# A hand-written order of steps replaced by another, with nine row subtractions moved from VectorE to GpSimd

## The chip, the cores and the metric

The kernel runs on one core of a Trainium2 chip. What counts is the device time of one execution in microseconds (us), the median of three runs. The engines of the core are TensorE (PE in the rows; its weight loads are PEld), VectorE (DVE), ScalarE (ACT), GpSimd (POOL) and SyncE (SP, which here only issues transfers).

## The reference

Four batches, eight heads of width 64 and 768 positions go through attention with a window of 128 and 4 sink positions; the 3072 rows that come out, 512 wide, go through a feed-forward layer with 2048 hidden units and a squared ReLU.

```python
scores = scale * np.matmul(q, k.transpose(0, 1, 3, 2))
keep = is_sink | in_window                      # rel in [0, window)
a = np.exp(np.where(keep, scores, -1e9) - max); a = a / (a.sum(-1) + 1e-9)
x = np.matmul(a, v)                             # (B, S, H*D) rows
h = np.maximum(x @ w_in, 0.0)
return h * h @ w_out
```

The weights arrive as float64, so that the kernel reads them as pairs of 32-bit words and makes of each row tile a high and a low part.

## The kernel before, in words

**Tiles.** A chunk is half a sequence: 384 positions, three query blocks of 128; there are eight chunks. A pair is two heads of one chunk; a chunk has four pairs. The pairs of chunks 0 and 1 are numbered 0 to 7.

**Attention of a pair.** Six score products (two heads, three blocks) go from TensorE into a bank of PSUM (`s`, line 277). VectorE scales, masks and takes a row bound (line 298), ScalarE takes the exponential and its sum (line 301). ScalarE adds a small number to the six sums and VectorE inverts them (309, 310). GpSimd multiplies the probabilities by the inverses, three instructions to a head (331), and packs the sink columns (344, 345). TensorE transposes the probabilities into three banks (`pt`, 408) and the sink columns into another (`pss`, 352); ScalarE or VectorE copies them to SBUF (`PTF`, 416, and `SK`, 359). TensorE makes the value product (`xo`, 462 and 465), ScalarE copies its high part (474), and VectorE subtracts for the low part (478).

**Feed-forward.** For each of 16 blocks of hidden units there are 12 matmuls into `ph` (524), ReLU and squares on ScalarE (535 to 540), a low part `gl` on VectorE (547), and 9 matmuls into `po` (562). Half a leg (one chunk, eight blocks) is cut into 32 quanta. For the first leg the order writes them as p0 to p31: two quanta of `ph`, then one of two thirds and one of a third of the `po` of the block before. p2 and p3 hold no matmul, so that p0 to p31 make eight `ph` and seven `po`.

**Rows of weights.** There are 32 row tiles; up to row 24, row 0 and the odd ones are of `w_in` (blocks 0, 1, 2, ...), the other even ones of `w_out` (blocks 0, 1, ...). VectorE makes a row in four steps: A (line 628), B (630), C (632, followed by ScalarE's copy of the high part, 637) and D, the low part (641): a subtraction of two tiles of SBUF, 128x512. A raw row lies in one of four buffers, and the load of row n+4 waits until step C of row n has read it.

**Order.** Up to the last step of that first leg the order on TensorE, VectorE, ScalarE, GpSimd and SyncE is written out by hand, as a string of small steps (`SCHEDULE`), and each engine does its share of them strictly in that order. A step's first letter says what it is, the first digit the pair: `s` scores, `x` the rest of a score, `e` inverses, `z` scaling of one head, `t` and `c` transposes and their copies, `k` and `K` the same for the sink columns, `m` value product, `X` and `L` its high and low part, `q` `v` `w` loads of queries and keys, of values and of a row, `A` to `D` a row's steps, `p` a quantum. A last `a` or `d` is the engine of a copy, `@n` the bank. `i` is a number of idle matmuls, 128x512 on zeros (line 684), whose result nobody reads. After the string the order comes from a planner that the change does not touch: from chunk 1's first feed-forward product on, TensorE's rows are the same in both kernels but for names and line numbers.

Of the kernel before, what the change touches and what calls it, by code (L numbers as in the profile page):

```python
# [50 lines left out]
K5a w12 D9 x701 C10 A11 m5 s702@3 B11 x702 s711@1 s712@0 D10 p17 p18 C11 A12 x712 k6@0 x711 B12 C12
t61@1 w13 D11 p19 w14 p20 w15 e7 v6 A13 c61a p21 D12 t62@2 K6a B13 c62a t60@1 z70 p22 A14 B14 z71
C13 w16 c60a p23 D13 w17 X5a p24 t70@1 C14 t72@3 A15 L5 p25 k7@0 w18 m6 c70a D14 c72a p26 B15 p27
C15 t71@1 X6a A16 c71a K7a L6 B16 p28 C16 v7 p29 D15 m7 p30 X7a p31 L7 D16
"""

# [6 lines left out]
def sink_window_attention_moe(  # L63
# [25 lines left out]
    with ExitStack() as fast:  # L89
# [18 lines left out]
        idle = ap1.tile([P, 512], BF16, tag="KS1", name="idle")  # L108
# [140 lines left out]
        def bank(b, name):  # L249
            pool, tag = ((ps_att, "att0"), (ps_att, "att1"), (ps_h, "h0"), (ps_h, "h1"), (ps_o, "o0"), (ps_o, "o1"), (ps_o, "o2"))[b]  # L250
            return pool.tile([P, 512], F32, tag=tag, name=name)
# [33 lines left out]
        def score_rest(c, p, hh, i):  # L285
            st = state[c, p]
            if "sm" not in st:
                st["sm"] = ap2.tile([P, 2, NQ], F32, tag="sm", name=f"sm_{c}_{p}")
                st["P"] = {}
# [15 lines left out]
        def inverses(c, p, heads=(0, 1)):  # L305
# [10 lines left out]
        def scale(c, p, *heads):  # L316
# [3 lines left out]
            rs = st["rs"]  # L320
            for hh in heads:
# [7 lines left out]
                for j in range(NQ):  # L329
# [117 lines left out]
        def value_products(c, p):  # L447
# [4 lines left out]
            st["xo"] = xo = ps_x.tile([P, 512], F32, tag="xo", name=f"xo_{c}_{p}")  # L452
# [20 lines left out]
        def x_high(c, p, eng):  # L473
            copies[eng](xT[c][0][:, p, :], state[c, p]["xo"][:, 0:TOK])

        def x_low(c, p):
            xh, xl = xT[c]
            nc.vector.tensor_tensor(xl[:, p, :], state[c, p]["xo"][:, 0:TOK], f32(xh[:, p, :]), op=ALU.subtract)
# [131 lines left out]
        AHEAD = 2  # L610
        raws = {}
# [380 lines left out]
```

## Time and profile before

| | us |
|---|---|
| median of 3 runs | 704.05 (703.09 to 704.42) |
| the profiled execution, its own time | 702.18 |
| its span, first to last instruction | 700.5 |
| TensorE busy in the span | 685.7 |
| VectorE, ScalarE, GpSimd busy | 426.5, 420.3, 228.7 |

The profile is of one execution, 1.87 us below the median. A busy TensorE is not one at its peak, as matmuls are pipelined and their ends modelled; where something is priced below, the distance between two starts is used where a row gives it.

### The profile page before, as it was taken

How to read it: one execution, taken by the hardware profiler on the slowest of the kernel's cores; microseconds unless marked ns; L12 is line 12 of the kernel's file. 1: busy time of each engine (PE TensorE's matmuls, PEld its weight loads, DVE VectorE, ACT ScalarE, POOL GpSimd, SP SyncE). 2: the span in 40 equal slices, each digit the busy share in tenths (PEclk: the TensorE clock that was granted, in tenths of full speed). 3: DMA queues.
4: the chain of work that ended last, by engine and by line, in shares of the span. 5: the costliest groups of instructions: out<-in, count | busy, mean ns of one | idle time of the engine just before them, and what ended most of it. 6: DMA issues, size and time to landing. Idle time of an engine off the chain costs nothing.

```text
span 700.5 us, 11632 instructions
## 1 busy us (share of the span) xinstructions
PE 685.7 (98%) x3862; PEld 595.4 (85%) x3862; DVE 426.5 (61%) x1141; ACT 420.3 (60%) x1216; POOL 228.7 (33%) x433
## 2 busy tenths in 40 slices
PE   8899999999999999999999999999999999999995
PEld 4687789998888889888888888888988889889994
DVE  6798899736657666566565656666555665542221
ACT  5786655645666776676667777666676544432221
POOL 4737500124553442343343344233244242200000
PEclk8999999999999999999999999999999999999998
DMA  7576676312424423332435432243433210010001
GB/s 205 157 216 193 199 231 212 128 36 68 128 70 140 107 79 106 107 118 77 119 97 149 117 105 78 77 149 85 114 104 84 66 44 15 1 46 1 1 0 51
DMA packets 47268, 71.51 MB, mean 102 GB/s; under 512 B 4384, under 2 KB 30752, under 8 KB 47200
## 3 DMA queue, kind: packets, MB, share of 16 engines
q1 hardware_dynamic: 47056, 70.55, 34.2%
q8 instruction: 33, 0.54, 0.3%
q14 instruction: 35, 0.29, 0.1%
q10 hardware_dynamic: 144, 0.13, 0.1%
HBM read 62.80 MB, written 7.86 MB: 101 GB/s over the span
## 4 chain that ended last, share of the span: by engine, by line
PE 93%; POOL 2%; DVE 1%; DMA 1%; SPq 1%; issue 0%; ACT 0%
PE ph L524 38%; PE po L562 37%; PE xo L462 6%; PE s L281 5%; PE pt L427 2%; POOL P L331 2%; PE s L277 2%; PE xo L465 2%; DMA kn<-in_k_dram 1%; PE pt L408 1%; SPq L205 0%; PE pss L352 0%; POOL PSK L344 0%; DVE t L630 0%; PE pss L367 0%
## 5 line engine op out<-in xcount | busy, mean ns | idle before, releaser
L524 PE MATMUL ph<-x,wi 128*128 128x384 f32 x1536 | 304.8, 340 | 0.0
L524 PEld LDWEIGHTS ph<-x,wi 128*128 128x128 f32 x1536 | 265.3, 188 | 8.8 <-issue 0.7
L562 PE MATMUL po<-wo,gh 128*128 128x512 f32 (+1 forms) x770 | 243.6, 397 | 0.0
L245 POOL TENSOR_TENSOR KS<-kn,KS 128x408 fp32r<-128x408 f32 (+1 forms) x48 | 58.6, 1221 | 314.9 <-ACT KS L244 314.9
L562 PEld LDWEIGHTS po<-wo,gh 128*128 128x128 f32 x770 | 136.4, 188 | 18.2 <-issue 0.2
L562 PE MATMUL po<-wo,gl 128*128 128x512 f32 x385 | 151.5, 394 | 0.0
L301 ACT ACTIVATE P<-P,nbs 128x264 f32<-128x264 f32 (+1 forms) x192 | 94.5, 492 | 78.5 <-DVE nbs L298 77.9
L298 DVE CUSTOM_DVE_ANT_0 P<-s,masks 128x264 f32<-128x264 f32 x160 | 67.8, 430 | 55.1 <-PE s L281 49.7
L543 DVE TENSOR_TENSOR ph<-ph,r 128x384 f32<-128x384 f32 x96 | 54.0, 563 | 76.7 <-ACT r L535 76.5
L331 POOL TENSOR_SCALAR P<-P,rs 128x136 f32<-128x136 f32 (+2 forms) x192 | 86.2, 465 | 33.1 <-DVE rs L310 27.8
L535 ACT ACTIVATE r<-ph 128x384 f32<-128x384 f32 x96 | 46.8, 487 | 77.4 <-PE ph L524 74.7
L547 DVE TENSOR_TENSOR gl<-ph,gh 128x384 fp32r<-128x384 f32 x128 | 71.1, 555 | 25.9 <-ACT ph L540 14.4
L562 PEld LDWEIGHTS po<-wo,gl 128*128 128x128 f32 x385 | 72.2, 188 | 15.9
L247 DVE TENSOR_TENSOR QS<-qn,QS 64x384 fp32r<-64x384 f32 x48 | 44.0, 917 | 26.4 <-ACT QS L246 26.0
L281 PE MATMUL s<-KS,QS 128*128 128x264 f32 (+1 forms) x288 | 56.9, 280 | 0.0
L326 POOL TENSOR_TENSOR P<-P 128x256 f32<-128x256 f32 (+1 forms) x48 | 48.3, 1007 | 24.9 <-ACT P L301 24.4
L281 PEld LDWEIGHTS s<-KS,QS 128*128 128x128 f32 x288 | 51.9, 188 | 5.0 <-DVE nbs L298 0.5
L538 ACT ACTIVATE gh<-r 128x384 fp32r<-128x384 f32 x96 | 50.3, 524 | 2.2
L433 DVE TENSOR_TENSOR PTF<-pt,halves 128x256 f32<-128x256 f32 x96 | 36.3, 419 | 22.1 <-PE pt L427 21.5
L462 PE MATMUL xo<-PTF,vn 128*64 128x256 f32 x448 | 45.9, 342 | 0.0
L462 PEld LDWEIGHTS xo<-PTF,vn 128*64 128x64 f32 x448 | 31.2, 136 | 16.0 <-issue 8.6
L244 ACT CAST KS<-kn 128x408 fp32r<-128x408 f32 (+1 forms) x48 | 28.3, 589 | 26.2 <-issue 13.2
(105 smaller groups left out, 645.4 us busy)
## 6 DMA issues: line engine op xcount, KB each, us to landing
raw<-in_moe_w_in_dram SPq DMA_DIRECT2D x16, 512.0 KB, 4.2
raw<-in_moe_w_out_dram SPq DMA_DIRECT2D x16, 512.0 KB, 4.1
half<-in_moe_w_in_dram SPq DMA_DIRECT2D x32, 256.0 KB, 2.6
half<-in_moe_w_out_dram SPq DMA_DIRECT2D x32, 256.0 KB, 3.6
kn<-in_k_dram SPq DMA_DIRECT2D x24, 272.0 KB, 4.1
qn<-in_q_dram SPq DMA_DIRECT2D x32, 192.0 KB, 3.5
out_dram<-ob SPq DMA_DIRECT2D x23, 256.0 KB, 2.3
kn<-in_k_dram SPq DMA_DIRECT2D x24, 204.0 KB, 3.5
```

Of the source, the lines that this page charges most:

```text
L245: nc.gpsimd.tensor_tensor(KS[:, 1, 0:nk], st["kn"][:, hh, 0:nk], f32(KS[:, 0, 0:nk]), op=ALU.subtract)
L281: nc.tensor.matmul(ps[:, 0:n], st["QS", hh][:, qcols], flat[:, a, c0 : c0 + n], start=(a == 0), stop=(a == 1))
L298: nc.vector.tensor_tensor_reduce(Pt[:, i, 0:n], ps[:, 0:n], mask[:, 0:n], -SCALE, BIG, ALU.add, ALU.min, nb)
L301: nc.scalar.activation(Pt[:, i, 0:n], Pt[:, i, 0:n], AF.Exp, bias=nb, scale=-1.0, accum_out=sm[:, i : i + 1])
L326: nc.gpsimd.tensor_tensor(Pt[:, j0:NQ, 0:P], Pt[:, j0:NQ, 0:P], Pt[:, j0:NQ, BS:BAND], op=ALU.add)
L331: nc.gpsimd.tensor_scalar(Pt[:, j, 0:n], Pt[:, j, 0:n], rs[:, hh, j : j + 1], 1.0, op0=ALU.mult, op1=ALU.mult)
L462: nc.tensor.matmul(xo[h * D : h * D + D, cols], lhsT, rhs, start=(n == 0), stop=False, skip_group_check=True)
L524: nc.tensor.matmul(ph[:, 0:TOK], wi_at(i, cc, fc), xt[:, cc, :], start=(m == 0), stop=(m == 3 * NCC - 1),)
L538: nc.scalar.activation(gh, r, AF.Square)
L543: nc.vector.tensor_tensor(ph[:, 0:TOK], ph[:, 0:TOK], r, op=ALU.mult)
L547: late = lambda: nc.vector.tensor_tensor(gl, ph[:, 0:TOK], f32(gh), op=ALU.subtract)
L562: nc.tensor.matmul(po[t][:, e], gt[:, ts_], wo[f][:, i, e], start=(f == f0 and j == 0), stop=(f == f1 - 1 and j == 2), skip_group_check=True,)
```

## The change

`SCHEDULE` is another string of about as many steps (348 in place of 349). The scores of pair 0 come first; attention of chunk 1 is taken earlier, and the rows' steps and the quanta later; of 29 idle matmuls 3 are left. Two lines of the new string:

```
i1@2 q0 i1@6 s000@0 q1 s001@7 x000 s010@6 s011@4 s002@0 x010 x001 s012@6 x011 s101@2 x002 s112@4 w0
A6 m4@0 p7 B6 w7 p8 C6 D5g D4d w8 A7 t52@3 t50@1 c52a A8 p9 B7 p10 K5d w9 B8 D6g w10 C7 C8 w11 X4d
```

Step D is done on GpSimd for the nine rows 0, 2, 3, 5, 6, 7, 13, 14 and 16. The small addition before the inverse goes from ScalarE to VectorE (pairs 0 to 6) or GpSimd (pair 7). Of the copies, those of `pt` 2,1 and `SK` of pairs 2 and 3 go from VectorE to ScalarE, and `pt` 2,0 and 5,1, `SK` of pairs 4 and 5 and the high parts of pairs 1, 4, 5 and 6 from ScalarE to VectorE. The value product may use any of the eight banks, scores and transposes the eighth too. Odd rows below 10 keep their working tile in a buffer of their own.

```diff
-            st["rs"] = rs = ap2.tile([P, 2, NQ], F32, tag="rs", name=f"rs_{c}_{p}_{heads[0]}")
-            nc.scalar.activation(rs[:, hs], st["sm"][:, hs], AF.Copy, bias=EPS)
+            st["rs"] = rs = ap2.tile([P, 2, NQ], F32, tag=f"rs{p % 2}", name=f"rs_{c}_{p}_{heads[0]}")
+            if eng == "a":
+                nc.scalar.activation(rs[:, hs], st["sm"][:, hs], AF.Copy, bias=EPS)
+            else:
+                engines[eng].tensor_scalar(rs[:, hs], st["sm"][:, hs], EPS, None, op0=ALU.add)
             nc.vector.reciprocal(rs[:, hs], rs[:, hs])
...
-        def value_products(c, p):
+        def value_products(c, p, b=7):
...
-            st["xo"] = xo = ps_x.tile([P, 512], F32, tag="xo", name=f"xo_{c}_{p}")
+            st["xo"] = xo = bank(b, f"xo_{c}_{p}")
...
-            t1 = ap2.tile([P, WR], I32, tag="t1", name=f"t1_{n}")
+            home = (wp, f"wo{6 + n % 4 // 2}") if n < EARLY_T and n % 2 else (ap2, "t1")
+            t1 = home[0].tile([P, WR], I32, tag=home[1], name=f"t1_{n}")
...
-            nc.vector.tensor_tensor(row[:, 1, :], f32(t1), f32(row[:, 0, :]), op=ALU.subtract)
+            lows = engines[(yield) or "d"] if n < EARLY else nc.vector
+            lows.tensor_tensor(row[:, 1, :], f32(t1), f32(row[:, 0, :]), op=ALU.subtract)
```

New functions for normalising behind the value product (`spread`, `widened`, `divided`) are not called: no step of the string names them.

**Place 1, TensorE, the first scores.** In a name the digits after `s` are the pair within its chunk, the head and the block; `kn`, `qn` are keys and queries. Before, from its third score on, with the first two rows of eight idle matmuls:

```order
L277 MATMUL s_0_0_1_175<-kn_0_162,qn_0_161 128x264
L277 MATMUL s_1_0_1_181<-kn_1_169,qn_1_168 128x264
L277 MATMUL s_1_0_0_190<-kn_1_169,qn_1_168 128x128
L277 MATMUL s_1_1_0_192<-kn_1_169,qn_1_168 128x128
L277 MATMUL s_0_0_2_194<-kn_0_162,qn_0_161 128x264
L277 MATMUL s_0_1_1_196<-kn_0_162,qn_0_161 128x264
L277 MATMUL s_0_1_2_198<-kn_0_162,qn_0_161 128x264
L277 MATMUL s_1_1_1_208<-kn_1_169,qn_1_168 128x264
L277 MATMUL s_1_1_2_216<-kn_1_169,qn_1_168 128x264
L277 MATMUL s_1_0_2_222<-kn_1_169,qn_1_168 128x264
L684 LDWEIGHTS idle
L684 MATMUL spare_228<-idle 128x512
```

The same place of the change, from its first score on:

```order
L284 MATMUL s_0_0_0_162<-kn_0_156,qn_0_155 128x128
L284 MATMUL s_0_0_1_169<-kn_0_156,qn_0_155 128x264
L284 MATMUL s_0_1_0_175<-kn_0_156,qn_0_155 128x128
L284 MATMUL s_0_1_1_177<-kn_0_156,qn_0_155 128x264
L284 MATMUL s_0_0_2_179<-kn_0_156,qn_0_155 128x264
L284 MATMUL s_0_1_2_186<-kn_0_156,qn_0_155 128x264
L284 MATMUL s_1_0_1_190<-kn_1_165,qn_1_164 128x264
L284 MATMUL s_1_1_2_194<-kn_1_165,qn_1_164 128x264
```

All six scores of pair 0 now stand ahead of pair 1's, and a single idle matmul follows the twelve scores.

**Place 2, TensorE, around the second quantum p1 of the first `ph`.** Before, p1 (the rows that read `x` and `wi`) and what follows:

```order
L408 MATMUL pt_0_0_649<-ident,P_0_0_479 128x128 x4
L524 MATMUL ph_0_634<-x_0_390,wi 128x384 x2
L524 MATMUL ph_0_634<-x_0_391,wi 128x384
L524 MATMUL ph_0_634<-x_0_390,wi 128x384 x2
L524 MATMUL ph_0_634<-x_0_391,wi 128x384
L277 MATMUL s_2_1_2_678<-kn_2_568,qn_2_567 128x264
L277 MATMUL s_2_0_0_681<-kn_2_568,qn_2_567 128x264
L277 MATMUL s_2_1_0_688<-kn_2_568,qn_2_567 128x264
L524 MATMUL ph_1_692<-x_0_390,wi 128x384 x2
```

The change:

```order
L568 MATMUL ph_0_551<-x_0_359,wi 128x384
L284 MATMUL s_2_0_2_658<-kn_2_504,qn_2_503 128x264
L284 MATMUL s_2_1_0_660<-kn_2_504,qn_2_503 128x264
L284 MATMUL s_3_0_0_662<-kn_3_533,qn_3_532 128x264
L284 MATMUL s_3_1_2_682<-kn_3_533,qn_3_532 128x264
L284 MATMUL s_3_0_1_687<-kn_3_533,qn_3_532 128x264
L284 MATMUL s_3_1_1_689<-kn_3_533,qn_3_532 128x264
L284 MATMUL s_3_0_2_691<-kn_3_533,qn_3_532 128x264
L421 MATMUL pt_0_0_709<-ident,P_0_0_422 128x128 x4
```

After p1 only seven scores are left, all in one piece (before, eleven, spread over the next quanta), and one group of pair 4's transposes.

**Place 3, GpSimd, the scalings of pairs 6 and 7.** `KS` is a subtraction for chunk 2, `P` the scalings, `PSK` the sink columns. Before, from pair 6's second head on:

```order
L331 TENSOR_SCALAR P_2_1_621<-P_2_1_621,rs_2_0_830 128x264 x3
L344 CAST PSK_139<-P_2_1_621 128x6x8
L345 TENSOR_TENSOR PSK_139<-P_2_1_621,PSK_139 128x3x8
L245 TENSOR_TENSOR KS_0_1_1570<-kn_0_1560,KS_0_1_1570 128x408
L245 TENSOR_TENSOR KS_0_0_1564<-kn_0_1560,KS_0_0_1564 128x408
L331 TENSOR_SCALAR P_3_0_920<-P_3_0_920,rs_3_0_1024 128x264 x3
```

The change, from pair 5's last sink columns to pair 6's first scaling:

```order
L358 TENSOR_TENSOR PSK_140<-P_1_1_468,PSK_140 128x3x8
L688 TENSOR_TENSOR wi<-t_3_629,wi 128x512
L252 TENSOR_TENSOR KS_0_0_1537<-kn_0_1533,KS_0_0_1537 128x408
L688 TENSOR_TENSOR wi<-t_5_759,wi 128x512
L252 TENSOR_TENSOR KS_0_1_1543<-kn_0_1533,KS_0_1_1543 128x408
L688 TENSOR_TENSOR wo_801<-t_6_772,wo_801 128x512
L688 TENSOR_TENSOR wi<-t_7_807,wi 128x512
L344 TENSOR_SCALAR P_2_0_667<-P_2_0_667,rs_2_0_765 128x264 x3
```

Step D of rows 3, 5, 6 and 7 (line 688) and both `KS` now stand ahead of pair 6's scalings.

## Rows read from the trace of the kernel before

**Rows 1.** Page of the profile, part 1, the engines' busy time: TensorE.

```profile
PE 685.7 (98%) x3862; PEld 595.4 (85%) x3862; DVE 426.5 (61%) x1141; ACT 420.3 (60%) x1216; POOL 228.7 (33%) x433
```

**Rows 2.** Windows: length, busy us (PE, PEld, DVE, ACT, POOL), granted clock.

```profile
0.00:24.27 24.27, 19.70 (x81) 10.24 (x81) 16.10 (x65) 13.56 (x46) 14.28 (x39) 0.86 0.67 194
24.27:40.88 16.61, 16.20 (x124) 11.49 (x123) 15.01 (x54) 13.88 (x45) 12.44 (x28) 1.00 0.63 197
40.88:93.50 52.62, 51.26 (x310) 42.16 (x310) 46.08 (x100) 37.93 (x95) 23.21 (x34) 1.00 0.66 196
93.50:131.00 37.50, 37.50 (x191) 34.15 (x190) 36.70 (x68) 20.37 (x42) 0.00 (x0) 1.00 0.54 180
```

**Rows 3.** Timeline of TensorE, 29 to 33 us: start, us, line, tile, count.

```profile
29.80 1.26 PE L408 MATMUL pt<-ident,P 128*128 128x128 f32 x10
30.90 0.38 PE L352 MATMUL pss<-ident,PSK 128*64 128x128 f32 x2
31.21 1.74 PE L277 MATMUL s<-kn,qn 64*128 64x264 f32 x12
32.88 1.30 PE L462 MATMUL xo<-PTF,vn 128*64 128x256 f32 x12
```

**Rows 4.** Timeline of TensorE, a value product of chunk 1 and what follows.

```profile
89.65 1.57 PE L462 MATMUL xo<-PTF,vn 128*64 128x256 f32 x16
...
91.43 0.62 PE L562 MATMUL po<-wo,gh 128*128 128x512 f32 x2
```

**Rows 5.** Chain of waits, two pieces of the saturated part: start, us, what.

```profile
95.79 2.08 PE po L562 x9
97.87 2.08 PE ph L524 x12
```

**Rows 6.** Timeline of all engines up to the first value product.

```profile
4.75 0.72 PE L277 MATMUL s<-kn,qn 64*128 64x128 f32 x2 [0.32 <-DMA kn<-in_k_dram]
...
6.76 0.40 ACT L301 ACTIVATE P<-P,nbs 128x128 f32<-128x128 f32 x1 [2.15 <-DVE nbs L298]
...
8.14 3.81 PE L277 MATMUL s<-kn,qn 64*128 64x128 f32 x14 [0.22 <-DMA kn<-in_k_dram]
...
11.89 3.60 PE L684 MATMUL spare<-idle 128*128 128x512 bf16 x8
...
13.58 1.47 POOL L331 TENSOR_SCALAR P<-P,rs 128x128 f32<-128x128 f32 x3 [8.62 <-DVE rs L310]
...
18.13 0.21 POOL L344 CAST PSK<-P 128x32 fp32r<-128x32 f32 x1
...
24.27 1.30 PE L462 MATMUL xo<-PTF,vn 128*64 128x256 f32 x12
```

**Rows 7.** Windows, two stretches; the column after POOL is the granted clock.

```profile
9.00:14.00 5.00, 5.00 (x15) 2.52 (x15) 3.93 (x17) 3.20 (x12) 0.42 (x2) 0.50 0.74 231
...
16.00:40.00 24.00, 21.66 (x154) 14.58 (x153) 19.90 (x73) 18.07 (x59) 19.45 (x43) 1.00 0.62 194
```

**Rows 8.** Groups of ScalarE, 0 to 93.5 us: count, busy us, mean ns.

```profile
L301 ACT ACTIVATE P<-P,nbs 128x264 f32<-128x264 f32 x40 | 20.3, 509 | 5.4 <-DVE nbs L298 5.2
L416 ACT COPY PTF<-pt 128x512 f32<-128x512 f32 x20 | 11.1, 584 | 1.8 <-PE pt L408 1.6 <-PE xo L462 0.2
...
L637 ACT CAST wi<-t 128x512 fp32r<-128x512 f32 x10 | 6.2, 620 | 1.0 <-DVE t L632 0.9
```

**Rows 9.** Groups of VectorE, 24 to 93.5 us: a masked score, a low part.

```profile
L298 DVE CUSTOM_DVE_ANT_0 P<-s,masks 128x264 f32<-128x264 f32 x28 | 11.2, 427 | 2.6 <-PE s L277 2.5
L641 DVE TENSOR_TENSOR wi<-t,wi 128x512 fp32r<-128x512 f32 x9 | 7.0, 782 | 0.5 <-ACT wi L637 0.5
```

**Rows 10.** Timeline of GpSimd and VectorE where two such subtractions meet.

```profile
64.39 1.07 POOL L245 TENSOR_TENSOR KS<-kn,KS 128x408 fp32r<-128x408 f32 x1
...
64.52 1.50 DVE L641 TENSOR_TENSOR wi<-t,wi 128x512 fp32r<-128x512 f32 x1
```

**Rows 11.** Timeline of GpSimd: three scalings among row steps of VectorE.

```profile
74.25 3.63 POOL L331 TENSOR_SCALAR P<-P,rs 128x264 f32<-128x264 f32 x3 [3.12 <-DVE rs L310]
```

More of the change, by code (lines that the diff above doesn't have):

```diff
@@ L319, in scale @@
             i0 = 1 if half == 0 else 0
-            rs = st["rs"]
+            rs = st.get("rs")
             for hh in heads:
@@ L328, in scale @@
                     )
-                for j in range(NQ):
+                for j in range(NQ) if not behind(c, p) else ():
                     n = P if j < j0 else (BS if c > 1 else BAND)
@@ L445, in values, with spread, widened, spread_copied @@
             x_low(c, p)
-        def value_products(c, p):
+        engines = {"g": nc.gpsimd, "d": nc.vector}
+        def spread(c, p, b):
+            st = state[c, p]
+            st["rb"] = rb = bank(b, f"rb_{c}_{p}")
+            for i in range(NQ):
+                nc.tensor.transpose(
+                    rb[:, i * P : (i + 1) * P], wide_rs[:, i].rearrange("p h d -> p (h d)"), ident
+                )
+        def widened(c, p, eng):
+            src = state[c, p]["rs"].rearrange("p h i -> p i h").unsqueeze(3).broadcast_to([P, NQ, 2, D])
+            if eng == "a":
+                nc.scalar.copy(wide_rs, src)
+            else:
+                engines[eng].tensor_copy(wide_rs, src)
+        def spread_copied(c, p, eng):
+            st = state[c, p]
+            if p % 2:
+                st["xs"] = xs_home
+            else:
+                st["xs"] = ap1.tile([P, TOK], F32, tag="eb", name=f"xs_{c}_{p}")
+            copies[eng](st["xs"], st["rb"][:, 0:TOK])
+        def divided(c, p):
+            st = state[c, p]
+            nc.vector.tensor_tensor(st["xs"], st["xo"][:, 0:TOK], st["xs"], op=ALU.mult)
+        def value_products(c, p, b=7):
             st = state[c, p]
@@ L473, in x_high, with x_low @@
         def x_high(c, p, eng):
-            copies[eng](xT[c][0][:, p, :], state[c, p]["xo"][:, 0:TOK])
-        def x_low(c, p):
+            src = state[c, p]["xs"] if behind(c, p) else state[c, p]["xo"]
+            copies[eng](xT[c][0][:, p, :], src[:, 0:TOK])
+        def x_low(c, p, eng="d"):
             xh, xl = xT[c]
-            nc.vector.tensor_tensor(xl[:, p, :], state[c, p]["xo"][:, 0:TOK], f32(xh[:, p, :]), op=ALU.subtract)
+            src = state[c, p]["xs"] if behind(c, p) else state[c, p]["xo"]
+            engines[eng].tensor_tensor(xl[:, p, :], src[:, 0:TOK], f32(xh[:, p, :]), op=ALU.subtract)
         pairs = [(c, p) for c in range(NCHUNK) for p in range(NPAIR)]
@@ L610, in sink_window_attention_moe @@
         AHEAD = 2
+        EARLY_T = 10
         raws = {}
@@ L708, in step @@
                 else:
-                    eng = arg[-1] if arg[-1] in "ad" else ""
+                    eng = arg[-1] if arg[-1] in "adg" else ""
                     c, p = pairs[int(arg[0])]
-                    more = [int(d) for d in arg[1:].rstrip("ad")]
+                    more = [int(d) for d in arg[1:].rstrip("adg")]
                     if b:
```

72 lines of the change are left out of this document (42 added, 30 removed).

## The prediction, written before the result was known

> **What bounds the kernel now.** I read the page first: TensorE is busy 98% of the span [rows 1]. Then I cut the span into stretches. From 93.50 us on TensorE is never idle (37.50 us of 37.50 in the window shown), at the full granted clock, and from there the change leaves its order alone; so what the change can give is how much earlier TensorE comes to the row that starts there, chunk 1's first feed-forward product. Ahead of it lie three stretches [rows 2]: up to 24.27 us, where the first value product starts [rows 6], a stretch of waiting on loads, softmax and scaling; up to 40.88, where the first quantum p0 starts, with VectorE 15.01, ScalarE 13.88 and TensorE 16.20 of 16.61 us busy; and up to 93.50, with TensorE 51.26 and VectorE 46.08 of 52.62. A busy TensorE is stretched by modelled ends, so I price its work by distances between starts.
>
> **Prices of TensorE's work** [rows 3 to 5]. Ten transposes take 30.90 - 29.80 = 1.10, 0.11 each; two sink transposes 0.31; six wide scores 32.88 - 31.21 = 1.67, 0.278 each. A value product of chunk 1 takes 91.43 - 89.65 = 1.78. Twelve `ph` matmuls take 2.08, nine `po` the same. From p0 to 93.50 before, the order has eight `ph` and seven `po` (31.2), eleven scores (3.06), twelve groups of four transposes (5.28), twelve sink transposes (1.86) and four value products (7.12): 48.5 in 52.62 us. So **4.1 us are lost** to waits there, beside what little the ends hide.
>
> **Step 1: the first value product.** Before, the first scaling starts at 13.58, though ScalarE's first exponential was at 6.76, because the exponentials of pair 1 stand among those of pair 0; its second head ends at 18.13; the value product starts at 24.27 [rows 6]. In between TensorE went through idle matmuls and waited for the scaling of pair 1, whose transposes stood ahead. In the change the six scores of pair 0 come first (place 1). Six exponentials in a row, two narrow at 0.40 and four wide at 0.509 [rows 6, 8], end at 6.76 + 2.8 = 9.6; I leave 0.6 for the inverse, so scaling starts at 10.2, 3.4 us earlier, and ends at 14.7. Then follow ten transposes, six scores of pair 3 (before, only two of them stood ahead) and two sink transposes: 1.1 + 1.7 + 0.3, which gives 17.8 at the full clock. At the low clock the same work costs about twice that: the fourteen score matmuls from 8.14 to 11.89, seven scores, took 0.53 each [rows 6], so 14.7 + 2.2 + 3.2 + 0.5 = 20.6. Nothing in the new order raises the clock early, so I take a value near the late end, **19.7**.
>
> **Step 2: p1.** From there ScalarE carries the attention of chunk 1, which the new order brings forward. Up to the high part of pair 3, which p1 reads, its new list holds 18 wide exponentials (9.2), one narrow (0.4), six copies of `pt` (3.5), three row copies (1.9) [rows 8], and five copies of `xo` and `pss`, for which I take the price of a wide exponential (2.5): 17.5 us. In the second stretch before it was busy 13.88 of 16.61 us, 84% [rows 2]; at that rate it needs 20.9. So the high part is there at 40.6 and **p1 ends at 41.6**. Bounds: without any gap 17.5, which ends p1 at 38.2.
>
> **Step 3: the rest.** After p1 TensorE has seven scores (place 2; 1.95), ten groups of transposes (4.4), the sinks (1.86), four value products (7.12) and 14 products (29.1): 44.4. I add the loss of before, 4.1, since the same engines feed the same steps. Chunk 1's first product then starts at 41.6 + 44.4 + 4.1 = **90.1 instead of 93.5: 3.4 us earlier**.
>
> **Edits that I cost at nothing.** The 22 idle matmuls after the first score are inside the stretches already counted. The addition before the inverse on VectorE, copies that change their engine and more buffers move work between engines that are each busy less than TensorE; their cover is the 84 to 90% of rows 2, and if it is gone, a copy of 0.584 [rows 8] delays the value product behind it by as much, eight such moves some 4 us at the very most, below nothing by as much where they relieve the engine that is late. The loads are issued in another order on SyncE, but each still waits for the buffer it fills; keys of chunk 1's second pair may now come a little before or after they are wanted, which I count in the loss.
>
> **Nine low halves on GpSimd.** The trace has no such instruction there. The nearest is a two-input subtraction of 408 columns, 1.07 us [rows 10]; for 512 columns I estimate 1.34 from it. VectorE saves 0.782 each [rows 9], but not all of it: where that GpSimd subtraction ran, VectorE's low half, started at 64.52, took 1.50 [rows 10], 0.72 more than the mean. After p1 seven of the nine are left. VectorE's 46.08 us [rows 2] become 46.08 - 7 x 0.782 - 6 x 0.427 (six masked scores fewer [rows 9]) + about 3 (six copies that it gains) = 41.0 in 48.5 us; with seven meetings at 0.72 it is 46.1, 95%. It still fits, barely; bounds are no meeting, 41.0, and a wait for the whole 1.34 each time, 50.4, about 2 us more than TensorE needs.
>
> The Trainium skill speaks against the move: SBUF — State Buffer (section SBUF: two separate sides) says that GpSimd and a VectorE operation with two SBUF inputs lock a shared port pair for the whole instruction, and the loser blocks. By that rule the upper bound is the one to reckon with, and the first rival below is what comes of it. The row at 64.52 agrees with it in kind: VectorE came 0.13 us after GpSimd and took twice its mean.
>
> **Sum.** Against the profiled execution: span 700.5 - 3.4 = 697.1, its own time 702.18 - 3.4 = 698.8. The median of three lies 1.87 above that execution, so 704.05 - 3.4 = **700.7**. Changes within 0.2%, 1.4 us, can't be told from none.
>
> **Rivals.** *The rows become the bound (slower or same).* GpSimd's new list has the low halves of rows 3, 5, 6 and 7 and two `KS` ahead of pair 6's scaling (place 3). Row 7's waits for step C of row 7 on VectorE; what is queued behind it is that scaling, and TensorE's transposes of pair 6 stand between the two halves of a `ph`. Three scalings took 3.63 where VectorE was full of row steps [rows 11]; with row 7's 1.34 a late step C can hold TensorE up to 5.0 us. For it speaks VectorE at 95%; against it that TensorE has about 17 us of work between p1 and those transposes (four and a half products and two value products' worth of attention). From 3.4 us of waiting on, the gain is gone; at 5.0 the time is 705.7.
>
> *The low clock stays (slower).* Before, the clock was 0.50 (1.2 GHz) from 9 to 14 us and full (2.4 GHz) from 16 on, after TensorE had worked from 8.14 almost without a gap through eight idle matmuls to 15.5 [rows 6, 7]. The change has one idle matmul there. From the first value product to p0 TensorE has 26 transposes, four sink transposes, twelve scores and two value products, some 9.8 us by rows 3 (3 us for the two value products is an estimate, below rows 4). Twice that is 9.8 more; ScalarE's pace leaves about 4.6 us of slack in the stretch, so 5.2 would reach the end: 705.9. Against it: at the low clock TensorE would itself be dense, as it was before the rise. It decides from about 8 us of work at the low level after 19.7.
>
> The Trainium skill's TensorE: Matmul & The Clock Gate (Part 1: The HAM clock gate) has it that the slow clock is the default and activity releases it. By that the missing idle matmuls are a loss; the trace agrees that eight of them came just before the rise.
>
> *Everything fits better.* ScalarE without gaps ends p1 at 38.2, and with half of the loss the end is 38.2 + 44.4 + 2 = 84.6, 8.9 us earlier: 695.2; with the whole loss 697.3.
>
> *It does nothing:* the string's end is set by the rows in both, 704.
>
> **Chances.** The forecast, 697.5 to 702.6, 0.50; better than that 0.15; the rows 0.22, most of it near no change; the low clock 0.10; nothing 0.03. Faster by over 0.2% has 0.50 + 0.15 + 0.04 = 0.69, no change 0.13, slower 0.18. The range goes from 696.0, between the two values of the better case, to 705.7, where the rows' rival ends; it leaves out most of the low clock's case and a little of the better one.
>
> **What would show it.** Right: pair 0's scaling starts near 10, the first value product near 19 to 20, p1 ends near 41 to 42, chunk 1's first product starts near 90, and TensorE runs full from there. Wrong: granted clock 0.50 beyond 20 us; TensorE waiting on GpSimd's scaling around the first half of the fifth `ph`; VectorE's low halves and steps B and C well above 0.8 us in the middle of the third stretch; ScalarE idle for long between 20 and 40 us because keys or scores are late.

## The result, and the profile after

The change is faster: 696.54 us (median of 4 runs, 694.24 to 697.05) beside 703.57 (4 runs, 703.02 to 704.42), ratio 0.9893, 95% interval 0.9867 to 0.9918. Taken again later beside other kernels it had 695.87 and a ratio of 0.9902 (0.9883 to 0.9920). The profiled execution took 697.05, with a span of 695.2. Forecast was 700.7, in a range from 696.0 to 705.7: the sign and the way of the gain were right, the gain was twice as large. The median lies 0.5 us inside the lower end of that range, and the median taken later 0.1 us below it.

The engines' busy time on the page of the changed kernel, which answers to [rows 1]:

```profile
PE 677.1 (97%) x3836; PEld 592.8 (85%) x3836; DVE 429.4 (62%) x1144; ACT 416.6 (60%) x1203; POOL 239.1 (34%) x443
```

Its windows, cut at its own first value product, end of p1 and chunk 1's first feed-forward product, answer to [rows 2] (busy us of PE, PEld, DVE, ACT and POOL, granted clock, share of the DMA, GB/s):

```profile
0.00:17.72 17.72, 12.91 (x64) 9.04 (x64) 11.75 (x60) 11.58 (x40) 10.92 (x36) 0.90 0.58 169
17.72:38.24 20.52, 19.46 (x143) 14.18 (x143) 19.97 (x69) 18.47 (x60) 17.27 (x34) 1.00 0.80 248
38.24:88.32 50.08, 45.71 (x282) 38.00 (x282) 47.07 (x91) 30.80 (x72) 32.80 (x41) 1.00 0.60 192
88.32:131.00 42.68, 42.68 (x217) 38.54 (x216) 40.41 (x78) 24.18 (x51) 0.14 (x1) 1.00 0.63 199
```

From 88.32 on TensorE is full, 42.68 of 42.68 us, as it was before from 93.50 on: the product comes 5.18 us earlier and the span is 5.3 shorter. That this one place decides is shown by all traces of this case: from the start of chunk 1's first product to the end of the span it is 607.0 us in the kernel before, 606.9 in the changed one, and 605.8 to 607.6 in the twelve below. The medians differ by 7.0 and not by 5.2 because the profiled execution of before lay 1.4 below its median and that of the changed kernel 0.5 above.

The timeline of the changed kernel, GpSimd and TensorE, at the four places that the forecast named, with the second head's scaling and the first transposes between the first two; the rows up to 17.72 answer to [rows 6]:

```profile
10.13 1.29 POOL L344 TENSOR_SCALAR P<-P,rs 128x128 f32<-128x128 f32 x3 [5.20 <-ACT P L308]
...
12.05 1.29 POOL L344 TENSOR_SCALAR P<-P,rs 128x128 f32<-128x128 f32 x3
...
14.18 1.96 PE L421 MATMUL pt<-ident,P 128*128 128x128 f32 x10
...
17.72 1.30 PE L504 MATMUL xo<-PTF,vn 128*64 128x256 f32 x12
...
37.01 1.30 PE L568 MATMUL ph<-x,wi 128*128 128x384 f32 x6
...
88.32 2.29 PE L568 MATMUL ph<-x,wi 128*128 128x384 f32 x12
```

The scaling starts at 10.13 (forecast 10.2), the first value product at 17.72 (19.7), p1 runs from 37.01 to 38.24 (its end forecast for 41.6), and chunk 1's product starts at 88.32 (90.1).

Where TensorE waits after p1: the timeline of the changed kernel between 45 and 61 us, TensorE first, then VectorE and GpSimd from 47 to 54 us (in brackets the idle time ahead of the row and its releaser):

```profile
47.39 0.45 PE L507 MATMUL xo<-SK,VS 128*128 128x384 f32 x1 [0.43 <-DVE SK L372]
...
50.56 1.09 PE L421 MATMUL pt<-ident,P 128*128 128x128 f32 x8 [0.96 <-DVE gl L591]
...
54.67 0.50 PE L606 MATMUL po<-wo,gh 128*128 128x512 f32 x1 [1.75 <-DVE wo L688]
...
60.25 0.50 PE L606 MATMUL po<-wo,gl 128*128 128x512 f32 x1 [0.87 <-DVE gl L591]
...
47.26 0.68 DVE L676 SCALAR_TENSOR_TENSOR t<-raw,t 128x512 int32<-128x512 int32 x1
...
49.63 0.40 DVE L674 TENSOR_SCALAR t<-raw 128x512 int32<-128x512 int32 x1
...
50.42 1.54 DVE L676 SCALAR_TENSOR_TENSOR t<-raw,t 128x512 int32<-128x512 int32 x1
...
53.93 0.68 DVE L688 TENSOR_TENSOR wo<-t,wo 128x512 fp32r<-128x512 f32 x1
...
50.14 1.27 POOL L688 TENSOR_TENSOR wi<-t,wi 128x512 fp32r<-128x512 f32 x1 [1.28 <-ACT wi L683]
```

Four waits make 4.0 us. The longest, 1.75, is for row 4's low part, which VectorE comes to at 53.93; its step B of row 6, started at 50.42 beside a low part on GpSimd, took 1.54 us, where such a step took 0.68 at 47.26. In the window of these 16 us VectorE, the third busy time, is the full one:

```profile
45.00:61.00 16.00, 11.99 (x71) 9.63 (x69) 15.87 (x27) 9.06 (x22) 7.13 (x6) 1.00 0.44 142
```

The low parts on GpSimd themselves cost what was estimated (1.34), by the groups of GpSimd from 38 to 131 us (count, busy us, mean ns):

```profile
L688 POOL TENSOR_TENSOR wo<-t,wo 128x512 fp32r<-128x512 f32 x4 | 5.6, 1408 | 9.2 <-ACT wo L683 9.2
L688 POOL TENSOR_TENSOR wi<-t,wi 128x512 fp32r<-128x512 f32 x4 | 5.1, 1282 | 4.6 <-ACT wi L683 4.6
```

### The profile page after: what moved, and what is told of

It is laid out like the page before. It is cut to its first block, busy times and chain, and to the rows that moved or that the text cites. A ratio compares the mean times of both kernels' runs of the same rounds, so it can differ in the third digit from the quotient of the medians.

```text
span 695.2 us, 11554 instructions
## 1 busy us (share of the span) xinstructions
PE 677.1 (97%) x3836; PEld 592.8 (85%) x3836; DVE 429.4 (62%) x1144; ACT 416.6 (60%) x1203; POOL 239.1 (34%) x443
## 4 chain that ended last, share of the span: by engine, by line
PE 91%; DVE 5%; DMA 1%; ACT 1%; issue 0%; POOL 0%; SPq 0%; DVEq 0%; POOLq 0%
PE ph L568 37%; PE po L606 37%; PE xo L504 6%; PE s L288 5%; PE pt L440 2%; PE xo L507 2%; DVE P L305 1%; DVE t L676 1%; PE s L284 1%; DMA kn<-in_k_dram 1%; DVE t L678 1%; DMA raw<-in_moe_w_in_dram 1%; DVE t L674 1%; PE pt L421 1%; POOL P L344 0%
## 5 line engine op out<-in xcount | busy, mean ns | idle before, releaser
L606 PEld LDWEIGHTS po<-wo,gl 128*128 128x128 f32 x385 | 72.2, 188 | 17.4 <-DVE gl L591 1.5
```

Source lines behind the costliest of these rows:

```text
L606: nc.tensor.matmul(po[t][:, e], gt[:, ts_], wo[f][:, i, e], start=(f == f0 and j == 0), stop=(f == f1 - 1 and j == 2), skip_group_check=True,)
```

## The experiments

All are compared with the kernel before in runs on the same chip. Each ratio is to the executions of before that were taken beside that kernel; their medians were 703.15 (runs 1 to 4), 703.34 (5, 6, 7 and 9) and 703.60 (8, 10, 11 and the change again). The places are read from one profiled execution of each kernel: the start of the first value product, of p1, and of chunk 1's first feed-forward product. For the old order p1 is left out, as other steps lie between it and the product there.

| kernel | median us | ratio to before (95%) | value product | p1 | product |
|---|---|---|---|---|---|
| before | 703.57 | | 24.27 | | 93.50 |
| the change | 696.54 | 0.9893 (0.9867 to 0.9918) | 17.72 | 37.01 | 88.32 |
| the change again | 695.87 | 0.9902 (0.9883 to 0.9920) | 16.59 | 36.12 | 87.25 |
| 1 all low parts on VectorE | 695.78 | 0.9895 (0.9878 to 0.9913) | 19.54 | 38.23 | 88.50 |
| 2 pair 0 later | 698.44 | 0.9937 (0.9919 to 0.9956) | 20.82 | 39.57 | 90.11 |
| 3 before, no idle matmuls | 703.58 | 1.0015 (1.0001 to 1.0030) | 24.83 | | 97.02 |
| 4 more idle matmuls at the start | 695.87 | 0.9891 (0.9874 to 0.9908) | 18.15 | 37.44 | 88.08 |
| 5 the code with the old order | 701.90 | 0.9981 (0.9971 to 0.9991) | 24.76 | | 96.59 |
| 6 old order, low parts on GpSimd | 707.30 | 1.0046 (1.0026 to 1.0065) | 25.73 | | 99.62 |
| 7 inverse's addition on ScalarE | 700.76 | 0.9960 (0.9945 to 0.9975) | 17.81 | 39.75 | 92.05 |
| 8 old order, addition on VectorE | 704.20 | 1.0008 (0.9997 to 1.0020) | 25.11 | | 95.86 |
| 9 relief between 45 and 60 us | 695.09 | 0.9880 (0.9862 to 0.9899) | 17.92 | 37.07 | 86.64 |
| 10 relief, low parts on VectorE | 696.78 | 0.9908 (0.9892 to 0.9924) | 19.20 | 37.75 | 88.60 |
| 11 relief, a sink's sum first | 695.33 | 0.9892 (0.9872 to 0.9911) | 17.77 | 36.72 | 87.58 |

The theory was that the front decides (pair 0 first, and a ScalarE and VectorE that are kept busy up to p1); its rivals that VectorE's row work after p1 sets the end, that GpSimd's low parts give or take, and that the clock does.

**The change again** (no edit).

> The changed kernel unchanged, to stand beside the three others: ratio 0.987 to 0.991, chunk 1's first feed-forward product at 88.0 to 88.7. If its first profile was a lucky one, the product comes at 89 or later and the ratio is over 0.992.

Ratio as expected; the product at 87.25 is earlier than that, with a value product at 16.59. Two executions of one kernel thus differ by 1.1 us at either place (why: last section). From p1 to the product they took 51.31 and 51.13 us; runs 2 and 4, whose order after p1 is the same, took 50.54 and 50.64. So a difference of 0.8 us or less in that last stretch can't be read from one trace, and in the front not even one of two microseconds.

**1. All low parts on VectorE.**

```diff
-x411 t21@3 D0g c21a A1
+x411 t21@3 D0d c21a A1
```

(so for D2, D3, D5, D6, D7, D13, D14 and D16.)

> The changed kernel with the low parts of all 17 rows on VectorE, nothing else moved. Five of the nine rows that GpSimd made stand between 38 and 61 us, where VectorE was busy 15.87 of 16 us (45 to 61) and waits of TensorE for it cost some 4 us. If GpSimd's low parts relieve VectorE there, five times 0.78 us more work comes back as lateness: chunk 1's first feed-forward product starts at 91 to 92 instead of 88.3 us and the median is 3 to 4 us above the changed kernel's 696.5. If the meetings eat the relief (VectorE's instructions that met a GpSimd low part took 1.3 to 1.9 us instead of about 0.8), the work added and the meetings saved cancel: the product starts at 88 to 89, the median is within 1 us of 696.5. A rival of its own: GpSimd's low parts do harm, and the product comes before 88.

The ratio is the changed kernel's. Its value product came later in this execution, in an order that differs up to there in nothing, and p1 with it. From p1 to the product it took 50.27 us, 0.3 to 1.0 less than the four traces with GpSimd's low parts, which is little beside their spread of 0.8. The timeline of this kernel between 45 and 61 us, TensorE and then a low part on VectorE, shows that TensorE's waits became one long and one short one:

```profile
52.20 1.32 PE L421 MATMUL pt<-ident,P 128*128 128x128 f32 x8 [2.32 <-DVE gl L591]
...
60.77 0.50 PE L606 MATMUL po<-wo,gl 128*128 128x512 f32 x1 [0.18 <-DVE gl L591]
...
53.48 0.68 DVE L688 TENSOR_TENSOR wi<-t,wi 128x512 fp32r<-128x512 f32 x1
```

A low part takes VectorE 0.68 there, about half of what it takes GpSimd. So in this order GpSimd's low parts are worth nothing that the times show, as the second expectation of this run had it.

**2. Pair 0 later.**

```diff
-s100@0 x012 x112 e0d x100 q2 s111@1 x101 x111 s102@5
+s100@0 x112 x100 s111@1 x101 x111 x012 e0d q2 s102@5
```

> The changed kernel with pair 0's last softmax and its inverses put behind four softmaxes of pair 1 (some 2 us of ScalarE's work at 0.50 each). If the early first pair is what the change earns with, the delay passes through: first scaling at 12 instead of 10.1, first value product at 19.5 instead of 17.7, high part of pair 3 about 1.8 later, chunk 1's first feed-forward product at 90 instead of 88.3, median about 698.4. If the row work on VectorE between 45 and 61 us sets the end, the delay is taken up there: product at 88.3 to 88.7 and the median within 0.5 us of 696.5.

The timeline of this kernel, GpSimd and TensorE, at the first scaling, the first value product and chunk 1's product:

```profile
13.06 1.54 POOL L344 TENSOR_SCALAR P<-P,rs 128x128 f32<-128x128 f32 x3 [8.11 <-DVE rs L323]
...
20.82 1.94 PE L504 MATMUL xo<-PTF,vn 128*64 128x256 f32 x12
...
90.11 2.29 PE L568 MATMUL ph<-x,wi 128*128 128x384 f32 x12
```

The first expectation holds. The edit cost more than four exponentials: the scaling waited for the reciprocal and came 2.9 us later. The value product came 3.1 to 4.2 later than in the two traces of the change, of which the clock may have a part (last section); 1.8 to 2.9 us are left at the product. The median, which hangs on no single trace, is 1.9 above the first and 2.6 above the second of the change's. The front passes through, for the most part.

**3. Before, without its 22 idle matmuls behind the first scores.**

```diff
-x112 B0 i8 A1 e0
+x112 B0 A1 e0
...
-z01 q3 i10 x210
+z01 q3 x210
...
-B3 A4 i4 t30@3
+B3 A4 t30@3
```

> The kernel before without its three groups of 8, 10 and 4 idle matmuls. If they hold the clock up, the granted clock falls to 0.50 in a stretch between 16 and 40 us and the median rises by 1 to 5 us over 703.6. If other matmuls hold it anyway, the clock column reads 1.00 from about 15 us on as before, and the time is within 0.7 us of 703.6 or, where the idle matmuls stood in front of work that was ready (22 at 0.22 to 0.43 us are 5 to 9 us of TensorE's queue), lower by up to 1 us.

The window of this kernel from 15 to 24 us (the column behind POOL is the granted clock):

```profile
15.00:24.00 9.00, 6.46 (x23) 3.75 (x21) 6.65 (x22) 5.53 (x20) 8.45 (x18) 0.50 0.69 207
```

In this execution the clock stayed at 0.50 (1.2 GHz) up to 29 us, against full clock from 16 us on before [rows 7], and the product came at 97.02. That this product is 3.5 us later than before is not the price of the idle matmuls: runs 5 and 8 have them all, rise to full clock at 14 to 15 us, and still come to the product at 96.59 and 95.86. Over 12 runs, leaving them out costs 0.15% (0.01 to 0.30), 1 us: in the traces at hand the clock rose earlier with them, but they were worth little.

**4. Seven idle matmuls at the start instead of two.**

```diff
-i1@2 q0 i1@6 s000@0
+i4@2 q0 i3@6 s000@0
```

> The changed kernel with seven idle matmuls instead of two at the start, where TensorE waits 3.4 us for the first keys. If the low clock at the start costs time, TensorE's first scores run at the high level some 2 us earlier, the first scaling and the first value product come 0.3 to 1.0 us earlier and chunk 1's first feed-forward product with them (87.3 to 88.0). If ScalarE's softmaxes set the pace of the start, these places stay within 0.2 us of 10.1, 17.7 and 88.3 and the median within 0.7 us of 696.5.

The value product at 18.15 is later than in both traces of the change, the product at 88.08 lies between theirs, and the ratio is the same. The granted clock reads 0.50 from 13 to 16 us here too: the low clock at the start is not shortened in this way.

**5. The code of the change with the table of before.** Here the string is that of the kernel before, and nothing else is edited.

```diff
-SCHEDULE = the string of the change
+SCHEDULE = the string of the kernel before
```

> The code of the change with the table of steps of before: only the new homes of the small tiles and the code that is not called are left of it. If the whole gain is in the table, this is the kernel before: ratio to before within 0.998 to 1.002, chunk 1's first feed-forward product at 93 to 94 us. If the tiles with homes of their own (the sums and their inverses by pair) give a part, the first scaling comes before 13 us and the ratio is under 0.998.

The code alone is worth 1.4 us, 2 at the most (0.9981, 0.9971 to 0.9991); the ratio just holds to the first expectation. The rest of the gain is in the table.

The product at 96.59 is later than the 93 to 94 expected, but this profiled execution took 704.75, 2.85 over the median of its own runs. Its clock fell again, which the clock of before did not do between 16 and 40 us [rows 7] (window of this kernel; the column behind POOL is the granted clock):

```profile
24.00:45.00 21.00, 20.81 (x146) 15.45 (x147) 17.12 (x61) 15.37 (x48) 13.98 (x32) 0.92 0.60 180
```

In windows of one microsecond it reads 0.50 from 26 to 28 us; in runs 6 and 8, of the same order, it reads 0.50 from 24 to 30 and from 25 to 27. So the product at 93.50, from which the forecast reckons, is that of a good execution of the old order; in runs 5 and 8 it comes at 96.59 and 95.86. In none of the traces of the new order does the column fall between 20 and 50 us.

**6. The old order with nine low parts on GpSimd.**

```diff
-q4 t00@6 D0 w3
+q4 t00@6 D0g w3
```

(so for D2, D3, D5, D6, D7, D13, D14 and D16.)

> As the run above, with the old table, and the low parts of the same nine rows on GpSimd. If GpSimd's low parts are worth something by themselves, VectorE's row steps come earlier and the ratio falls under 0.998 (a gain of 1.5 to 3 us, product at 91 to 92). If the meetings of GpSimd and VectorE eat it, as the run with all low parts on VectorE says, the ratio stays within 0.998 to 1.002; if the meetings cost more than the 0.78 us that each low part spares VectorE, the ratio is over 1.002.

It is slower, by 0.46% against before and by 0.65% against run 5, as the third expectation had it, but not by meetings alone. A wait in the timeline of this kernel that run 5 doesn't have, GpSimd, then VectorE, then TensorE (its lines stand one above those of the change):

```profile
77.89 3.63 POOL L343 TENSOR_SCALAR P<-P,rs 128x264 f32<-128x264 f32 x3 [3.12 <-DVE rs L322]
...
82.43 1.40 POOL L343 TENSOR_SCALAR P<-P,rs 128x264 f32<-128x264 f32 x3
...
84.39 1.29 POOL L687 TENSOR_TENSOR wi<-t,wi 128x512 fp32r<-128x512 f32 x1
...
85.71 1.47 DVE L673 TENSOR_SCALAR t<-raw 128x512 int32<-128x512 int32 x1 [3.37 <-POOL wi L687]
87.11 0.55 DVE L521 TENSOR_TENSOR x<-xo,x 128x384 fp32r<-128x384 f32 x1
...
87.71 2.52 PE L503 MATMUL xo<-PTF,vn 128*64 128x256 f32 x16 [2.12 <-DVE x L521]
...
99.62 0.68 PE L567 MATMUL ph<-x,wi 128*128 128x384 f32 x3
```

The low part of a row of `w_in` stands behind two heads of scaling on GpSimd (77.89 to 83.8) and ends at 85.68. VectorE's next step A waits 3.37 us for it, since it goes into the working tile that this low part still reads; behind it stands the low part of a value product, and TensorE waits 2.12 us for that; its product is 3.0 later than in run 5. It is the reverse of the rival that I feared for the change: there a scaling was to wait behind low parts on GpSimd, here a low part waits behind scalings. In the new order VectorE waited for GpSimd in this way once, 1.2 us.

**7. The addition ahead of the inverses on ScalarE again.**

```diff
-s100@0 x012 x112 e0d x100
+s100@0 x012 x112 e0 x100
```

(so for e0 to e6, and for e7, which the change has on GpSimd.)

> The changed kernel with the additions ahead of the inverses on ScalarE again, which in the first 40 us is busy over 90 per cent. If ScalarE's pace sets the first 40 us and each small addition costs it its 0.2 us and a wait for the sums, the first value product comes 0.2 to 0.5 later than 17.7 and the median rises by 0.5 to 1.5 us. If not, places and median stay within 0.3 and 0.7 us of the changed kernel's.

This was the surprise: 700.76, 4.2 and 4.9 us above the two medians of the change, product at 92.05. Waits in this kernel up to 96 us, VectorE for ScalarE's addition and ScalarE for VectorE's masked scores (us in total, times, longest):

```profile
DVE rs L323 <- ACT rs L320: 8.8, 8, 1.9
...
ACT P L308 <- DVE nbs L305: 7.2, 12, 1.2
```

The second of these waits in the change:

```profile
ACT P L308 <- DVE nbs L305: 4.1, 6, 1.2
```

One of the eight waits, pair 2's, in the timeline of this kernel, ScalarE and then VectorE:

```profile
16.83 0.51 ACT L308 ACTIVATE P<-P,nbs 128x264 f32<-128x264 f32 x1
...
18.86 0.40 ACT L308 ACTIVATE P<-P,nbs 128x128 f32<-128x128 f32 x1 [1.04 <-DVE nbs L305]
...
19.83 0.52 ACT L308 ACTIVATE P<-P,nbs 128x264 f32<-128x264 f32 x1
...
20.34 0.20 ACT L320 ACTIVATE rs<-sm 128x6 f32<-128x6 f32 x1
...
18.74 0.43 DVE L305 CUSTOM_DVE_ANT_0 P<-s,masks 128x264 f32<-128x264 f32 x1
...
20.57 0.19 DVE L323 RECIPROCAL rs<-rs 128x6 f32<-128x6 f32 x1 [1.39 <-ACT rs L320]
```

Pair 2's last exponential is that of 16.83, so its sums are there by 17.4. The addition stands in ScalarE's queue behind two exponentials of pair 3, the high part of pair 0's value product and a third exponential of pair 3, and comes at 20.34. VectorE has done its last masked score ahead of the reciprocal at 19.2 and stands still for 1.39 us; the eight waits of this kind make 8.8 us. The masked scores behind the reciprocal come late, and ScalarE waits for them in turn, 7.2 us in place of 4.1. With the addition on VectorE both instructions run as soon as VectorE is there: the list of VectorE's waits in the change has none for them. TensorE's first value product was not later here (17.81); p1 was, by 2.7 and 3.6 us. From the value product to p1 it took 21.94 us, and 18.55 to 19.53 in the eight other traces of the new order, so this is more than one execution's luck.

**8. The old order with the addition on VectorE:** run 5 and this edit.

```diff
-B1 e1 s210@0
+B1 e1d s210@0
```

(so for e0 to e7.)

> The code of the change with the old table, and the additions ahead of the inverses on VectorE. In the new order VectorE's reciprocal waited 8.8 us for ScalarE's addition when it was put back there. If the addition's engine is worth that by itself, the old order gains 2 to 4 us too (ratio 0.993 to 0.996). If it matters only where the reciprocal stands right behind the last softmax of its pair, as in the new order, the old order, whose reciprocals did not wait for ScalarE, stays at 0.997 to 1.001.

The second expectation holds: 1.0008, and beside run 5 it even costs a little, as the two intervals do not meet. In the old order (before and run 5) the list of VectorE's waits has none for the addition. Of the two orders, the edit is worth something in the new one only.

**9. Relief between 45 and 60 us.** Three copies from VectorE to ScalarE, row 4's low part earlier.

```diff
-C4 D3g A5 K4d B5 C5 e6d k5@7 A6 m4@0
+C4 D3g A5 K4a B5 C5 e6d k5@7 D4d A6 m4@0
...
-D5g D4d w8
+D5g w8
...
-p10 K5d w9
+p10 K5a w9
...
-w11 X4d
+w11 X4a
```

> The changed kernel with three small copies between 45 and 60 us (two of the sink's sums, one high part; 0.54 us each on VectorE) moved to ScalarE, which was busy 9.06 of 16 us there, and with row 4's low part two row steps earlier on VectorE. If VectorE's work between 45 and 61 us holds the end back, TensorE's waits there (1.75 for row 4's low part, 0.96 and 0.87 for the relu's low part, 0.43 for a sink's sum) fall by 1.5 to 2.5 us, chunk 1's first feed-forward product comes at 86 to 87 and the median is 1.5 to 2 us under the changed kernel's. If only the early front decides, the waits move elsewhere, the product stays at 88 to 88.6 and the median within 0.7 us.

The timeline of this kernel, TensorE, and then VectorE and GpSimd where a row's step A meets a low part:

```profile
47.84 0.44 PE L507 MATMUL xo<-SK,VS 128*128 128x384 f32 x1 [1.30 <-ACT SK L372]
...
51.16 1.09 PE L421 MATMUL pt<-ident,P 128*128 128x128 f32 x8 [1.14 <-DVE gl L591]
...
86.64 2.28 PE L568 MATMUL ph<-x,wi 128*128 128x384 f32 x12
...
49.13 1.52 DVE L674 TENSOR_SCALAR t<-raw 128x512 int32<-128x512 int32 x1
...
49.07 1.29 POOL L688 TENSOR_TENSOR wi<-t,wi 128x512 fp32r<-128x512 f32 x1 [1.28 <-ACT wi L683]
```

Step A took 1.52 us beside the low part, and 0.40 in the change at 49.63. TensorE's wait of 1.75 is gone, that for a sink's sum has grown from 0.43 to 1.30, now for ScalarE; between 45 and 61 us TensorE waits 2.6 us in place of 4.0. From p1 to the product it takes 49.57 us, 1.0 to 1.7 less than the four traces with the change's order there: the row work on VectorE did hold TensorE up after p1. The product comes at 86.64, as expected, 0.6 and 1.7 earlier than in the two traces of the change. The median is 0.8 and 1.5 us below the two of the change, less than the 1.5 to 2 that were expected. The ratio is the lowest of all, but its interval overlaps those of the change: that it beats the change is not shown by the times.

**10 and 11. The relief with all low parts on VectorE,** and then with the sink's sum ahead of a row's copy on ScalarE:

```diff
-k4@1 C4 D3d A5 K4a B5
+k4@1 K4a C4 D3d A5 B5
```

> The last kernel of the run before (three copies on ScalarE, row 4's low part earlier) with the low parts of all 17 rows on VectorE. If a low part on GpSimd costs VectorE as much by what it delays there as the 0.68 us that it spares (row steps that met one took 1.4 to 1.9 us instead of 0.45 to 0.68), chunk 1's first feed-forward product comes at 85.5 to 87 against 86.6 with them, and the median within 0.7 us of 695.1 or under it. If GpSimd's help is needed now that VectorE is still busy 15.8 of 16 us between 45 and 61, five low parts more are 3.4 us: product at 89 to 90, median about 698.

> As the run above, with the sink's sum of one value product put ahead of a row's copy in ScalarE's queue: in the run before it stood behind that copy (46.81, 0.60 us) and TensorE waited 1.30 us for it. If that wait is on the path, the product comes 0.4 to 0.7 us earlier than in the run above; if VectorE's steps are late next anyway, it comes within 0.2 us of it.

Both take 50.85 us or 0.01 more from p1 to the product, 1.3 more than run 9. By these traces GpSimd's low parts help a little with the relief, where without it they cost 0.3 to 1.0 (run 1); but run 9's 49.57 is one trace, four traces of one order are 0.8 apart, and the intervals of the three ratios overlap, so that neither worth is shown to differ from nothing. Neither expectation held in full. In run 11 the wait for the sink's sum fell from 1.7 to 1.2, and the path took the same time: VectorE's steps were late next. Run 9 has the lowest median of the versions tried.

## Why the prediction was right in kind and off in size

**What bounds.** Right. The gain is how much earlier TensorE comes to chunk 1's first product: 5.18 of 5.3 us of the span.

**Step 1, the first value product: mis-sized by 2.0 us.** The scaling was right to 0.1 us. I took 19.7 for the value product, near the end of my bounds at which the low clock lasts through it. It came at 17.72, near the early bound, 17.8, but not by that bound's way. GpSimd was through with both heads' scaling at 13.34, where I had 14.7, so that the transposes started at 14.18; that is 0.5 of the 2.0. They ran in part at the low clock still, and the clock rose in time for the second half of the work; that is the other 1.5, and luck in part, as other executions of this order come to the value product anywhere from 16.59 to 19.54 (last section). Windows of the change, the column behind POOL is the granted clock; they answer to [rows 7]:

```profile
13.00:14.00 1.00, 1.00 (x6) 0.76 (x4) 0.97 (x6) 0.54 (x3) 0.79 (x3) 0.50 0.80 224
16.00:17.00 1.00, 1.00 (x11) 0.87 (x11) 0.81 (x5) 0.82 (x3) 1.00 (x4) 1.00 0.82 229
```

Before 13 us the column is not to be trusted (last section).

**Step 2, p1: mis-sized by 1.4 us beside that, and this is the step that failed.** I took ScalarE's pace of the old order, 84%. It was busy 18.47 of 20.52 us, 90%, and VectorE 19.97, 97%, up from 90% of its stretch before [rows 2]: the fullest engine of the stretch was VectorE, and not ScalarE, which I let carry it. Run 7 shows what one edit has to do with that: the addition ahead of the inverse, which I listed among the **edits that I cost at nothing**, "between engines that are each busy less than TensorE". Moved back it costs 4.2 to 4.9 us, and 2.7 to 3.6 are there at p1. I had weighed the work that it moves, 0.2 us each, and not that the addition stands behind other pairs' work in ScalarE's queue while VectorE, strictly in order, stands still. Nor is it the addition alone: in the old order, where other steps stood between the last softmax and the reciprocal, it gains nothing (run 8). My bound for such moves, "some 4 us at the very most, below nothing by as much", was about the size of it.

**Step 3, the rest: mis-sized by 1.6 us to the other side.** I added the loss of before, 4.1. From the end of p1 to the product it took 50.08 in place of 48.5, a loss of 5.7. Of this 4.0 are the waits between 45 and 61 us, where VectorE was at 15.87 of 16; run 9 took 1.6 to 1.7 out of the stretch by three copies and one step.

**Nine low halves on GpSimd.** The price per instruction was right (1.34 forecast; 1.28 for `w_in`, 1.41 for `w_out` measured), and VectorE at 95% was right: 47.07 of 50.08, 94%. That the saving and the meetings nearly cancel in the new order is what the two terms of the forecast come to, and run 1 bears it out. What I had not worked out is GpSimd's own queue, by which the same edit loses some 4 us in the old order (run 6).

The rule of the Trainium skill that I put against this edit, in SBUF — State Buffer (section SBUF: two separate sides), is that of a GpSimd operation and a VectorE operation with two SBUF inputs the one that comes first keeps the shared port pair for its whole instruction. The trace agrees in kind: at 50.14 and 50.42 in the change GpSimd took its 1.27 and VectorE 1.54 for a step with two such inputs that takes 0.68 at 47.26. That the change gained all the same does not speak against it: run 1 shows that the edit did not make the gain.

**The sum.** 90.1 less 2.0, less 1.4, plus 1.6 is 88.3. The other 1.9 us between the 3.4 that were forecast for the median and the 7.0 measured, beyond the 1.8 at the product, lie in the two profiled executions: I carried the gain over from one that lay lower in its runs than that of the change. The errors of steps 1 and 2 have one sign and that of step 3 the other: without it the median would have been 694.9, below the range. That the range holds the result is luck to that extent.

**The rivals.** *The rows become the bound*: true in part. It took 4 us, but at row 4's low part and the relu's, not at pair 6's scaling, which started on time (60.64; TensorE waited for it under 0.2 us), and the front had gained more. *The low clock stays*: not in the trace of the change. It was full from 16 us on without the eight idle matmuls, and run 3 gives them 1 us. In run 1, in the same order up to there, it rose at 18 us only. Nor does the clock make the gain: over its executions the mean granted clock is 0.9955 for the change and 0.992 to 0.993 for the kernel before, while run 3 had 0.9888 beside 0.9932 and was 1 us slower; at that price, an estimate from these means, the clock is 0.5 to 0.8 of the 7.0 us. No run holds the clock alike in both orders. *Everything fits better*: the median is there, 695.2 to 697.3, by the way named there for p1 (38.24; 38.2 without gaps), but with a larger loss behind it, not half of it. *It does nothing*: no.

**What the parts are worth.** Shown by taking away: the addition on VectorE 4.2 to 4.9 us in the new order (run 7); pair 0's early end 1.9 to 2.6 for 2.9 us of the first scaling (run 2). Low parts on GpSimd nothing that the times show in the new order, idle matmuls at most 2 us in the old. Tiles and code without the table at most 2 us (run 5). How the copies and the order of chunk 1's attention share the rest was not tried apart.

## What to carry to other kernels

A small instruction that sits between two engines that work in order is priced by what waits behind it on both queues, not by its own length: in one order 0.2 us of addition on the wrong engine cost 8.8 us of VectorE's time and 4 us of the kernel's, and in another order nothing. An engine's pace of before is no constant of a new order; take the bound without gaps as seriously, and ask which wait made the gaps. Before a gain is put down to an edit, undo that edit alone: the low parts on GpSimd look like relief in the diff; in the new order they are worth nothing that the times show, and in the old one they cost some 4 us. And before a place in one trace is put down to an edit, take several executions of one order: here they lie up to 3 us apart in the front, and 0.8 us after it.

## What the runs showed of the hardware

The clock rises at different times in executions of the same order. Ten transposes of pair 0 that take 1.31 us at the full clock in one execution of the change took 2.39 in run 10, in which the granted clock reads 1.00 in every window from 8 to 22 us: the column is not to be trusted ahead of the first rise or fall that it shows. The timeline of TensorE in that execution of the change, run again:

```profile
13.49 1.31 PE L421 MATMUL pt<-ident,P 128*128 128x128 f32 x10
...
16.59 1.30 PE L504 MATMUL xo<-PTF,vn 128*64 128x256 f32 x12
```

And in run 10, with the same instructions up to there:

```profile
14.55 2.39 PE L421 MATMUL pt<-ident,P 128*128 128x128 f32 x10
...
19.20 1.30 PE L504 MATMUL xo<-PTF,vn 128*64 128x256 f32 x12
```

In the traces with the change's order up to there, the first value product comes anywhere between 16.59 and 19.54 (run 1).

The clock can fall again later. In the second profile of the change TensorE was busy 0.44 of 2 us, and then ran at the low level for the most part of 4 us (windows; the column behind POOL is the granted clock); in the first, with nearly the same waits (0.96 and 1.75 us beside 0.99 and 1.75), it did not fall.

```profile
52.00:54.00 2.00, 0.44 (x2) 0.39 (x3) 1.97 (x5) 1.06 (x3) 0.36 (x1) 1.00 0.34 87
54.00:58.00 4.00, 4.00 (x14) 3.39 (x13) 4.00 (x6) 1.73 (x5) 0.99 (x1) 0.57 0.62 192
```

The Trainium skill's TensorE: Matmul & The Clock Gate (Part 1: The HAM clock gate) has the low clock as the default and activity as what releases it. The traces agree in kind; that one execution falls back and another doesn't is not told by what the two traces show.
